# Attention projections in two row halves for units 4 to 15, one product for numerator and denominator in units 8 and 9, on one Trainium2 core

## The chip, the core and the metric

One of the eight cores of a Trainium2 chip runs the whole program. Its engines are TensorE (PE, with the loads of its stationary operand shown as PEld), VectorE (DVE), ScalarE (ACT), GpSimd (POOL) and SyncE (SP, which here issues DMAs). TensorE writes to PSUM, which has eight banks of 512 fp32 values in each of 128 partitions. The metric is the time on the device of one execution, in microseconds, as the median of several.

## The reference

Three layers follow one another: linear attention with positive random features, a gated MLP (in the code "moe"), and a soft mixture of experts ("moe2"). The change is in the first.

```
x = q * D**-0.25  (and k)                 # 4 batches, 8 heads, 576 tokens, D = 64
h = x @ omega.T - sum(x*x)/2              # 128 features
phi = exp(h - max(h)) / sqrt(128)
kv = phi(k).T @ v ;  z = sum(phi(k), tokens)
out = (phi(q) @ kv) / (phi(q) @ z + 1e-6)
x = out as 2304 tokens x 512
x = (sigmoid(x @ w_gate) * (x @ w_val)) @ w_out      # 1536 hidden
out = soft mixture of 8 experts with 4 slots each    # w1, w2 of 1024 hidden
```

## The kernel before

**Units.** A unit is two heads of one batch; there are 16. q and k come transposed, so a unit's tile has the two heads' 64 dimensions on 128 partitions and 1152 token columns (512 of k, a mixed tail tile of 64 of k and 64 of q, 512 of q). `chunk_proj` (L534) makes features of one or two tiles of 128 tokens: the token tile is the stationary operand and `obf` moves, omega of both heads as a block diagonal of 128 x 256, half of it zeros. One product gives both heads' 128 features. DVE then takes, per head and tile, the minimum of 128 features with the square sum added (`tensor_tensor_reduce`), ACT the exponential. The features lie in `HK`, `HT`, `HQ`, one buffer each. Five such calls make a unit.

**Precision.** For units 0 to 9 (`N_PROJ`, `N_NUM` = 10) these products are fp32; one appears as two records of TensorE, each streaming its columns twice. From unit 10 on q, k and omega are split into a high and a low fp32r part (`prep_qk`, L509), and `three` (L414) makes three passes of one record.

**After the projection.** `chunk_kv` (L559) sums features times v over the tokens, in 10 products a unit; v has ones beside it, so a head's 128 columns hold kv and z. `chunk_qT` (L573) turns the q features by TensorE: two calls with four 128 x 128 transposes and a third with two of the tail tile's 64 q rows (partitions 64 to 127). `chunk_num` (L589) is called for each half of the tokens (288). For units 0 to 9 it makes the denominators of both heads in one bank and the numerators in another, each by two products of 64 columns' width that write the two halves of the partitions. From unit 10 on one product of 128 columns gives numerator and denominator of a head.

**Banks.** `bank` (L496) hands out PSUM. While the first four units run, six tags serve attention; from then on (`wide[0]` false) attention and the moe2 chunks share the tag `fl` with two banks (`NFL = 2`). `ga`, `va` and `o0` to `o3` belong to the MLP.

**Order.** Nothing is issued directly. Each call is recorded by `Plan.add` (L136), and `Plan.schedule` (L213) runs a list schedule over the whole program with estimated costs (`cost`, L179), which fixes each engine's order, and for some operations the engine. A key taken from the job's due time and a lead per stream sets the priority. Each engine then runs its list in order and waits on semaphores. An operation on `fl` that finds no bank free is parked and offered again when one comes free.

**Stages.** Units 0 to 3 come first. Then the MLP runs in groups of steps over blocks of tokens (`GROUPS`, L32); a step is 12 matmuls each for `ga`, `va` and the `o` banks, fp32r, 512 columns. Units 4 to 7 lie among the first group, 8 to 11 among the second and third, 12 to 15 among the fourth; their outputs feed the MLP's later blocks. In the first two groups the MLP's weights are also converted from 64-bit floats (`convert`, L683) on ACT, DVE and POOL. `step_chunks` (L626) orders a unit's chunks: the sums of unit u, with the projection of unit u+1 in between.

Of the kernel before, what the change touches and what calls it, by code (L numbers as in the profile page):

```python
# [46 lines left out]
    "hqk": ("DVE", "ACT"), "lqk": ("POOL", "DVE"), "hqt": ("ACT", "DVE"),  # L47
# [9 lines left out]
N_PROJ = 10  # L57
# [28 lines left out]
HOP = 0.16  # L86

# [11 lines left out]
class Plan:  # L99


    def __init__(self, nc):
        self.eng = {"PE": nc.tensor, "ACT": nc.scalar, "DVE": nc.vector, "POOL": nc.gpsimd, "SP": nc.sync}
        self.ops = []
        self.tiles = {}
        self.tags = {}
        self.t = 0.0
        self.lead = {}
        self.floor = 0.0
        self.floors = []  # L110
        self.hist = {}

# [23 lines left out]
    def add(self, alts):  # L136
        _, method, args, kw = alts[0]
        outs = [kw[k] for k in ("out", "accum_out") if k in kw]
        ins = [v for k, v in kw.items() if k not in ("out", "accum_out") and hasattr(v, "tensor")]
        rest = [a for a in args if hasattr(a, "tensor")]  # L140
        if "out" not in kw and rest:
            outs.append(rest.pop(0))
        ins += rest
        i = len(self.ops)
# [24 lines left out]
        self.ops.append((alts, self.t - lead, preds, used, outs, ins, self.lead.get("lazy")))  # L169
# [9 lines left out]
    def cost(self, eng, method, kw, outs, ins):  # L179


        o = outs[0] if outs else None
# [30 lines left out]
    def schedule(self):  # L213
# [13 lines left out]
        dyn_of = [None] * n  # L227
        left = {}
        for tag, info in self.tags.items():
            gens = info["gens"]  # L230
            if info["dyn"]:
                for g, acc in enumerate(gens):
                    left[tag, g] = len(acc)
                    for a in acc:
                        dyn_of[a] = (tag, g)
# [86 lines left out]
        while ev:  # L322
            now = ev[0][0]
            while ev and ev[0][0] <= now + 1e-9:
# [3 lines left out]
                elif kind == 2:  # L328
                    d = dyn_of[x]
                    left[d] -= 1  # L330
                    if left[d] == 0:
                        room[d[0]] += 1
                        for p in parked[d[0]]:
                            offer(p)
                        parked[d[0]] = []
            for e in E:
                while free_at[e] <= now + 1e-9:
# [5 lines left out]
                    d = dyn_of[i]  # L343
                    if d and d not in live:
                        if room[d[0]] == 0:
                            if i not in parked[d[0]]:
                                parked[d[0]].append(i)
                            continue
                        room[d[0]] -= 1
                        live.add(d)  # L350
# [20 lines left out]
                    if d:  # L371
# [5 lines left out]
    def issue(self):  # L377
        for _, _, (e, method, a, k) in self.schedule():
            getattr(self.eng[e], method)(*a, **k)  # L379


def body(ctx, tc, nc, qkT, tok, von, omT, wall, phi, w1, w2, ident_d, srep_d, rrep_d, mask_d, out):
# [71 lines left out]
    q0, q1 = region(0, F32), half_region(0, F32)  # L454
# [3 lines left out]
    QT = KV = XK = XQ = obh = obl = None  # L458

    def split_regions():  # L460

        nonlocal QT, KV, XK, XQ, obh, obl
        g0, g1 = region(0, F32R), half_region(1, F32R)
        QT = carve(g0, 0, [2, 2, S])
        KV = carve(g0, 2304, [2, 2, 128])
        XK = carve(g0, 2816, [2, 640])
        XQ = carve(g1, 0, [2, 512])
        obh = carve(g1, 1024, [256])
        obl = carve(g1, 1280, [256])
        hi_of(obh, obf, ("DVE",))  # L470
        lo_of(obl, obf, obh, ("DVE",))
# [6 lines left out]
    HK = carve(g4, 0, [4, 2, M])  # L478
    HQ = carve(g4, 1024, [4, 2, M])
    HT = carve(g4, 2048, [1, 2, M])  # L480
# [5 lines left out]
    MX = [carve(g4, 3730 + 8 * k, [2, 4]) for k in range(6)]  # L486
# [22 lines left out]
    def prep_qk(u, kind):  # L509
# [3 lines left out]
        if u == N_PROJ and kind == 0:  # L513
            split_regions()
        x, c, t, n = ((XK, slice(0, 640), 0, 5), (XQ, slice(640, 1152), 5, 4))[kind]
        src = QKTs[u % 2][:, c]
# [16 lines left out]

    def chunk_proj(u, i):  # L534

        if u >= NU:
            return
        x, c0, nt, hb, g0 = ((XK, 0, 2, HK[:, 0:2], 0), (XK, 256, 2, HK[:, 2:4], 4), (XK, 512, 1, HT, 8),
                             (XQ, 0, 2, HQ[:, 0:2], 10), (XQ, 256, 2, HQ[:, 2:4], 14))[i]
        ps = bank()  # L540
        psv = ps.rearrange("p (t m) -> p t m", t=2)
        for t in range(nt):
            c = slice(c0 + 128 * t, c0 + 128 * t + 128)
            if u < N_PROJ:
                PE.matmul(psv[:, t], QKTs[u % 2][:, 640 * (i > 2) + c0 + 128 * t:][:, 0:128], obf, start=True, stop=True)
            else:
                three(psv[:, t], (x[:, 0, c], x[:, 1, c]), (obh, obl))
        n = 2 * nt
        sq = SQ[:, g0:g0 + n]
        flat = ps.rearrange("p (g m) -> p g m", m=M)[:, 0:n, :]  # L550
        hv = hb.rearrange("p t h m -> p (t h) m")
        low = turn(MX, "mx")[:, 0, 0:n]
        for g in range(n):
            DVE.tensor_tensor_reduce(out=hv[:, g], in0=flat[:, g], in1=sq[:, g:g + 1].to_broadcast([128, M]),
                                     scale=1.0 / 16.0, scalar=BIG, op0=ALU.add, op1=ALU.min, accum_out=low[:, g:g + 1])
        for g in range(n):
            ACT.activation(out=hv[:, g], in_=hv[:, g], func=AF.Exp, scale=-1.0, bias=low[:, g:g + 1])

    def chunk_kv(u):  # L559

        ps = bank()[:, 0:256].rearrange("p (h c) -> p h c", h=2)
        for h in range(2):
            for t in range(NT):
                k = HK[:, t, h, :] if t < 4 else HT[:, 0, h, :]
# [8 lines left out]
    def chunk_qT(u, i):  # L573
        ps = bank().rearrange("p (h n) -> p h n", h=2)
        n = (256, 256, 64)[i]
        for h in range(2):
            if i == 2:
                PE.transpose(ps[:, h, 0:64], HT[64:128, 0, h, :], ident[64:128, 64:128])
                continue
            for t in range(2):  # L580
                PE.transpose(ps[:, h, 128 * t:128 * t + 128], HQ[:, 2 * i + t, h, :], ident)
        if u < N_NUM:
            copy(QTF[:, :, 256 * i:256 * i + n], ps[:, :, 0:n], SITE["hqt"])
            return
        qh, ql = (QT[:, l, :, 256 * i:256 * i + n] for l in range(2))
        hi_of(qh, ps[:, :, 0:n], SITE["hqt"])
        lo_of(ql, ps[:, :, 0:n], qh, ("DVE",))

    def chunk_num(u, half):  # L589
# [4 lines left out]
        if u < N_NUM:  # L594
# [8 lines left out]
        else:  # L603
            pn = []
            for h in range(2):
                ps = bank()[:, 0:HALF]
                pn.append(ps)
                three(ps, (KV[:, 0, h, :], KV[:, 1, h, :]), (QT[:, 0, h, c:c + HALF], QT[:, 1, h, c:c + HALF]))
                ACT.activation(out=R[num[h]], in_=ps[den[h]], func=AF.Ln, bias=den_b[den[h]])
# [16 lines left out]
    def step_chunks(u):  # L626
# [11 lines left out]
        def last():  # L638
            chunk_proj(v, 4)
            prep_qk(u + 2, 0)  # L640

        c = [kv, P(0), lambda: chunk_qT(u, 0), P(1), lambda: chunk_qT(u, 1), lambda: chunk_qT(u, 2), P(2),
             lambda: chunk_num(u, 0), P(3), lambda: chunk_num(u, 1), last]
        own = (0, 2, 4, 5, 7, 9)
# [444 lines left out]
    chunk_proj(0, 0)  # L1089
    prep_first(2, 5)  # L1090
    prep_qk(0, 1)
    chunk_proj(0, 1)
    chunk_proj(0, 2)
    SP.dma_start(out=TOK, in_=tok[1])
    SP.dma_start(out=Vs[1], in_=von[1])
    chunk_proj(0, 3)
    chunk_proj(0, 4)
# [186 lines left out]
```

## Time and profile before

| | us |
|---|---|
| median of 3 runs | 703.87 |
| lowest, highest | 703.55, 704.65 |
| the profiled execution: its span, first to last instruction | 702.4 |
| PE busy | 678.3 |
| PEld busy | 543.9 |
| DVE busy | 445.7 |
| ACT busy | 443.1 |
| POOL busy | 301.3 |

The profiled execution has no time of its own beside its span. All computing instructions are issued at line L379, so groups are told apart by the names of tiles: `fl<-g,g` is attention work, `ga`, `va` and `o` with `XT,w` or `gt,w` are the MLP. Busy time of PE is modelled at its ends, so the starts of successive records tell more than their durations.

### The profile page before, as it was taken

The numbers are of one execution on the slowest core, as the hardware profiler recorded it, in microseconds if no ns is written. First come the engines' busy times: TensorE is split into PE (matmuls) and PEld (weight loads), VectorE is DVE, ScalarE is ACT, GpSimd is POOL, SyncE is SP. The second block draws the span as 40 slices with busy tenths as digits, with TensorE's granted clock in tenths as the row PEclk, the third lists the DMA queues.
The fourth block names the chain that finished last, engine by engine and source line by source line (L and its number), as shares of the span: only waits on it lengthen the run. The fifth ranks groups of instructions, "written<-read, shape, count | busy, mean of one in ns | idle before, by whom it ended". The sixth has DMA issues, their size and how long they took to land.

```text
span 702.4 us, 12029 instructions
## 1 busy us (share of the span) xinstructions
PE 678.3 (97%) x4095; PEld 543.9 (77%) x4095; DVE 445.7 (63%) x1292; ACT 443.1 (63%) x987; POOL 301.3 (43%) x255
## 2 busy tenths in 40 slices
PE   8999999999989999999999999999999999999993
PEld 6677667777767788788888888778888788998662
DVE  4898997899997554657476765555454335766221
ACT  5999898888777565856567674654444444765021
POOL 0356545546454444644444444354444444642000
PEclk9999999999999999999999999999999999999998
DMA  7878777677866335443333334469422228557897
GB/s 279 297 253 308 249 229 255 227 257 271 267 238 201 123 114 206 148 133 108 133 135 132 90 115 142 127 231 330 166 91 90 91 83 281 168 162 250 320 407 235
DMA packets 50124, 139.47 MB, mean 199 GB/s; under 512 B 5520, under 2 KB 11152, under 8 KB 50064
## 3 DMA queue, kind: packets, MB, share of 16 engines
q1 hardware_dynamic: 45456, 121.94, 51.9%
q10 hardware_dynamic: 4608, 16.78, 6.9%
q8 instruction: 32, 0.52, 0.3%
q14 instruction: 28, 0.23, 0.1%
HBM read 124.54 MB, written 14.16 MB: 197 GB/s over the span
## 4 chain that ended last, share of the span: by engine, by line
PE 67%; DVE 4%; issue 3%; ACT 2%; DMA 2%; POOL 1%; POOLq 0%; ACTq 0%; DVEq 0%
PE o L379 19%; PE ga L379 18%; PE va L379 18%; PE fl L379 12%; DVE x2T L379 2%; DMA ws<-wscr 1%; DVE g L379 1%; DVE ga_a L379 1%; ACT ga_a L379 1%; DMA g<-in_wall 1%; POOL w L379 1%; ACT g L379 0%; ACT XT L379 0%; ACT gt L379 0%; ACT x2T L379 0%
## 5 line engine op out<-in xcount | busy, mean ns | idle before, releaser
L379 POOL TENSOR_TENSOR w<-ws,w 128x512 fp32r<-128x512 f32 x141 | 188.3, 1336 | 235.7 <-ACT w L379 132.5
L379 PE MATMUL ga<-XT,w 128*128 128x512 f32 (+1 forms) x720 | 169.4, 377 | 1.8 <-DVE ga_a L379 1.0
L379 PE MATMUL va<-XT,w 128*128 128x512 f32 (+1 forms) x720 | 167.6, 376 | 1.2 <-DVE ga_a L379 1.2
L379 PE MATMUL o<-gt,w 128*128 128x512 f32 (+1 forms) x720 | 165.3, 374 | 0.9 <-ACT w L379 0.8
L379 PEld LDWEIGHTS ga<-XT,w 128*128 128x128 f32 x720 | 123.8, 189 | 28.1 <-issue 3.0
L379 PEld LDWEIGHTS va<-XT,w 128*128 128x128 f32 x720 | 123.5, 189 | 27.1 <-issue 3.7
L379 PEld LDWEIGHTS o<-gt,w 128*128 128x128 f32 x720 | 123.6, 189 | 25.1 <-issue 2.6
L379 ACT ACTIVATE g<-g 128x128 f32<-128x128 f32 (+3 forms) x340 | 121.1, 415 | 18.9 <-DVE g L379 12.9
L379 ACT ACTIVATE w<-ws 128x512 fp32r<-128x512 f32 x107 | 67.3, 629 | 61.9 <-issue 19.8
L379 PE MATMUL fl<-g,g 128*128 128x128 f32 (+2 forms) x514 | 87.8, 343 | 3.2 <-DVE g L379 2.1
L379 PEld LDWEIGHTS fl<-g,g 128*128 128x128 f32 (+1 forms) x514 | 61.8, 179 | 22.5 <-issue 6.6
L379 ACT ACTIVATE ga_a<-ga_a 128x512 f32<-128x512 f32 (+1 forms) x120 | 70.2, 585 | 12.6 <-DVE ga_a L379 11.5
L379 ACT ACTIVATE ga_a<-ga 128x512 f32<-128x512 f32 (+1 forms) x60 | 33.2, 554 | 65.4 <-PE ga L379 65.3
L379 DVE CUSTOM_DVE_ANT_0 g<-fl,g 128x128 f32<-128x128 f32 x242 | 56.9, 286 | 19.5 <-PE fl L379 19.0
L379 DVE SCALAR_TENSOR_TENSOR ga_a<-ga,ga_a 128x512 f32<-128x512 f32 (+1 forms) x60 | 38.2, 636 | 46.4 <-ACT ga_a L379 46.1
L379 DVE CAST w<-ws 128x512 fp32r<-128x512 f32 x55 | 23.8, 432 | 67.8 <-PE ga L379 38.1
L379 ACT ACTIVATE x2T<-g 128x512 f32<-128x512 f32 x72 | 45.9, 670 | 5.8 <-DVE x L379 5.7
L379 DVE TENSOR_SCALAR x2T<-x2T 128x512 f32<-128x512 f32 (+1 forms) x72 | 47.7, 670 | 0.9 <-ACT x2T L379 0.8
L379 DVE TENSOR_TENSOR ga_a<-va,ga_a 128x512 f32<-128x512 f32 (+1 forms) x60 | 38.0, 634 | 15.3 <-ACT ga_a L379 11.9
L379 POOL TENSOR_TENSOR XT<-g,XT 128x288 fp32r<-128x288 f32 (+2 forms) x46 | 31.3, 690 | 32.0 <-ACT XT L379 29.5
L379 ACT ACTIVATE ga_a<-ga_a,one_b 128x512 f32<-128x512 f32 (+1 forms) x60 | 40.8, 679 | 1.2
L379 DVE TENSOR_TENSOR g<-fl,g 64x288 f32<-64x288 f32 (+3 forms) x57 | 27.6, 485 | 15.5 <-ACT g L379 12.5
(200 smaller groups left out, 752.6 us busy)
## 6 DMA issues: line engine op xcount, KB each, us to landing
ws<-wscr SPq DMA_DIRECT2D x42, 512.0 KB, 3.6
ws<-wscr SPq DMA_DIRECT2D x78, 256.0 KB, 2.8
g<-in_wall SPq DMA_DIRECT2D x36, 512.0 KB, 4.9
g<-in_von SPq DMA_DIRECT2D x16, 640.0 KB, 5.1
wscr<-x SPq DMA_DIRECT2D x36, 256.0 KB, 4.5
g<-in_qkT SPq DMA_DIRECT2D x15, 576.0 KB, 4.8
g<-in_tok SPq DMA_DIRECT2D x15, 576.0 KB, 5.0
g<-in_w ACTq DMA_DIRECT2D x16, 512.0 KB, 5.2
```

What stands on the lines that cost most here:

```text
L379: getattr(self.eng[e], method)(*a, **k)
```

## The change

From unit 4 on (`ROWS = 4`), the four full tiles of k (and of q) of both heads are projected in one call as eight fp32 products with 64 rows each: head 0 from partitions 0 to 63, head 1 from 64 to 127, 128 columns each, in two banks, one for each head. The tail tile stays one block-diagonal product. The split of q, k and omega for units 10 to 15 is dropped; their projections are fp32. Units 0 to 3 keep the old calls under new names. Features have two sets of buffers that alternate by unit (the second in the region `g1b`). The tail tile is transposed whole, and only its q columns are copied. Units 8 and 9 make numerator and denominator of a head as one fp32 product, in two banks. `together` records several products as one bundle for the planner: they are ordered as a block, and need all their banks free at once. An operation on `fl` now also parks behind one with an earlier key. Three prices of the planner change.

```diff
+TURN = 0.2
+ROWS = 4
+WHOLE = 8
+    def together(self, calls, first=(), then=()):
+        self.bundle = []
+        calls()
+        parts, self.bundle = self.bundle, None
+        self.place([(parts[0][0][0], "together", (), {"parts": parts})],
+                   [o for _, outs, _ in parts for o in outs] + list(then),
+                   [i for _, _, ins in parts for i in ins] + list(first))
...
             if o.ap[0][1] == 64:
-                return max(n / 600.0, 0.21) / 2 + 0.02, False
-            return (0.416 if ins[0].ap[0][1] == 64 else max(0.222, n / 600.0)), False
+                return max(n / 600.0, 0.21) / 2 + 0.12, False
+            return (max(0.222, n / 600.0) / 2 if ins[0].ap[0][1] == 64 else max(0.222, n / 600.0)), False
...
             if method == "tensor_tensor_reduce":
-                return 0.16 + ni / 960.0, False
+                return 0.075 + ni / 960.0, False
...
-                    if d and d not in live:
-                        if room[d[0]] == 0:
+                    fresh = [d for d in dyn_of[i] if d not in live]
+                    if fresh:
+                        tag = fresh[0][0]
+                        first = any(ops[q][1] < ops[i][1] for q in parked[tag])
+                        if room[tag] < len(fresh) or first:
...
-        if u >= N_PROJ:
-            hi_of(x[:, 0, :], src, SITE["hqk"])
-            lo_of(x[:, 1, :], src, x[:, 0, :], SITE["lqk"])
...
+        def products():
+            for t in range(nt):
+                if nt < 4:
+                    PE.matmul(both[:, t].rearrange("p h m -> p (h m)"), x[:, 128 * t:128 * t + 128], obf,
+                              start=True, stop=True)
+                    continue
+                for h in range(2):
+                    r = slice(64 * h, 64 * h + 64)
+                    PE.matmul(ps[h][:, t], x[r, 128 * t:128 * t + 128], obf[r, 128 * h:128 * h + 128],
+                              start=True, stop=True)
+        plan.together(products, [SQ[:, g0:g0 + 2 * nt]], [hb])
...
-                PE.transpose(ps[:, h, 0:64], HT[64:128, 0, h, :], ident[64:128, 64:128])
+                PE.transpose(ps[:, h, 0:128], HTs[u % 2][:, 0, h, :], ident)
...
-        if u < N_NUM:
+        if u < WHOLE:
...
+                    if u < N_NUM:
+                        PE.matmul(pn[h], KVF[:, h], QTF[:, h, c:c + HALF], start=True, stop=True)
...
+        if v < ROWS:
+            c = [kv, P("K0"), qT[0], P("K1"), qT[1], qT[2], P("T"), num[0], P("Q0"), num[1], last]
+        else:
+            c = [kv, P("K"), qT[0], qT[1], qT[2], P("T"), num[0], num[1], last]
```

## Rows read from the trace of the kernel before

**Rows 1.** The page: busy time of each engine, share of the span, instructions

```profile
PE 678.3 (97%) x4095; PEld 543.9 (77%) x4095; DVE 445.7 (63%) x1292; ACT 443.1 (63%) x987; POOL 301.3 (43%) x255
```

**Rows 2.** Stretches: length, busy time of each engine, granted clock, DMA

```profile
core 0: us, PE busy (x) PEld busy (x) DVE busy (x) ACT busy (x) POOL busy (x), PEclk, DMA share, GB/s
0.00:40.00 40.00, 36.41 (x194) 27.20 (x194) 26.28 (x138) 30.63 (x88) 11.21 (x16) 1.00 0.80 282
60.00:160.00 100.00, 98.18 (x499) 71.91 (x499) 86.56 (x265) 87.78 (x212) 50.92 (x46) 1.00 0.75 249
160.00:200.00 40.00, 36.93 (x166) 29.61 (x165) 38.62 (x63) 30.21 (x58) 20.97 (x15) 1.00 0.74 253
200.00:470.00 270.00, 268.83 (x1467) 220.67 (x1466) 166.53 (x502) 176.99 (x384) 124.97 (x105) 1.00 0.44 146
470.00:640.00 170.00, 168.82 (x1020) 146.28 (x1020) 90.84 (x185) 87.70 (x167) 80.80 (x63) 1.00 0.51 167
```

**Rows 3.** PE in order of time (start, length, names, shapes, count): bare groups

```profile
469.82 2.88 PE L379 MATMUL ga<-XT,w 128*128 128x512 f32 x12
472.54 2.88 PE L379 MATMUL va<-XT,w 128*128 128x512 f32 x12
```

**Rows 4.** PE in order of time: transposes, then two old projection tiles in fp32

```profile
188.28 0.60 PE L379 MATMUL fl<-ident,g 128*128 128x128 f32 x4
188.63 3.02 PE L379 MATMUL va<-XT,w 128*128 128x512 f32 x12
191.49 1.02 PE L379 MATMUL fl<-g,g 128*128 128x256 f32 x4
192.16 3.12 PE L379 MATMUL o<-gt,w 128*128 128x512 f32 x12
195.12 0.60 PE L379 MATMUL fl<-ident,g 128*128 128x128 f32 x4
```

**Rows 5.** PE in order of time: features times v, then fp32r projection tiles

```profile
342.70 2.39 PE L379 MATMUL fl<-g,g 128*128 128x128 f32 x20
344.85 2.98 PE L379 MATMUL ga<-XT,w 128*128 128x512 f32 x12
347.66 0.88 PE L379 MATMUL fl<-g1b,g 128*128 128x256 f32 x6
348.38 2.91 PE L379 MATMUL va<-XT,w 128*128 128x512 f32 x12
351.13 0.60 PE L379 MATMUL fl<-ident,g 128*128 128x128 f32 x4
```

**Rows 6.** PE in order of time, products of 64 columns' width; a group of their loads

```profile
244.70 1.19 PE L379 MATMUL fl<-g,g 128*64 128x288 f32 x8
245.82 3.02 PE L379 MATMUL va<-XT,w 128*128 128x512 f32 x12
248.68 0.88 PE L379 MATMUL fl<-g1b 128*128 128x256 f32 x6
...
L379 PEld LDWEIGHTS fl<-g,g 128*64 128x64 f32 x120 | 6.2, 135 | 11.1 <-issue 5.6 <-DVE g L379 2.2 <-ACT g L379 1.6
```

**Rows 7.** PE in order of time: transposes of a 64-row half

```profile
235.47 2.99 PE L379 MATMUL va<-XT,w 128*128 128x512 f32 x12
238.40 0.33 PE L379 MATMUL fl<-ident,g 64*128 64x64 f32 x2
238.66 3.01 PE L379 MATMUL o<-gt,w 128*128 128x512 f32 x12
241.51 0.52 PE L379 MATMUL fl<-g1b,g 128*128 128x256 f32 x3
```

**Rows 8.** Groups on DVE and ACT (busy us, mean ns); PE's waits (us, times, longest)

```profile
L379 DVE CUSTOM_DVE_ANT_0 g<-fl,g 128x128 f32<-128x128 f32 x242 | 56.9, 286 | 19.5 <-PE fl L379 19.0
L379 DVE TENSOR_TENSOR g<-fl,g 64x288 f32<-64x288 f32 x24 | 10.9, 454 | 5.8 <-ACT g L379 3.1 <-PE ga L379 2.3
L379 ACT ACTIVATE g<-fl,den_b 64x288 f32<-64x288 f32 x24 | 12.0, 499 | 1.6 <-PE fl L379 0.9
PE fl L379 <- DVE g L379: 5.2, 9, 1.8
```

More of the change, by code (lines that the diff above doesn't have):

```diff
@@ L46 @@
 SITE = {
-    "hqk": ("DVE", "ACT"), "lqk": ("POOL", "DVE"), "hqt": ("ACT", "DVE"),
+    "hqt": ("ACT", "DVE"),
     "hx": ("ACT", "DVE"), "lx": ("POOL", "DVE"), "hg": ("DVE", "ACT"),
@@ L56 @@
 T0 = -60
-N_PROJ = 10
+N_SPLIT = 10
 N_NUM = 10
@@ L111, in __init__ @@
         self.hist = {}
+        self.bundle = None
+    def together(self, calls, first=(), then=()):
[5 more added lines that the diff above has]
+                   [i for _, _, ins in parts for i in ins] + list(first))
     def tile(self, pool, shape, dtype, tag, bufs=1, dyn=False):
@@ L143, in add, with place @@
         ins += rest
+        if self.bundle is not None:
+            self.bundle.append((alts[0], outs, ins))
+        else:
+            self.place(alts, outs, ins)
+    def place(self, alts, outs, ins):
         i = len(self.ops)
@@ L179, in cost @@
     def cost(self, eng, method, kw, outs, ins):
+        if method == "together":
+            return TURN * (kw["parts"][0][2][0].ap[0][1] == 64) + sum(self.cost(eng, a[1], a[3], o, i)[0] for a, o, i in kw["parts"]), False
         o = outs[0] if outs else None
@@ L226, in schedule @@
         nv = n
-        dyn_of = [None] * n
+        dyn_of = [[] for _ in range(n)]
         left = {}
@@ L234, in schedule @@
                     for a in acc:
-                        dyn_of[a] = (tag, g)
+                        dyn_of[a].append((tag, g))
                 continue
@@ L328, in schedule @@
                 elif kind == 2:
[L329 to L335, printed above, removed]
+                    for d in dyn_of[x]:
+                        left[d] -= 1
+                        if left[d] == 0:
+                            room[d[0]] += 1
+                            for p in parked[d[0]]:
+                                offer(p)
+                            parked[d[0]] = []
             for e in E:
@@ L342, in schedule @@
                     backlog[p[0]] -= self.cost(p[0], p[1], p[3], ops[i][4], ops[i][5])[0]
-                    d = dyn_of[i]
-                    if d and d not in live:
-                        if room[d[0]] == 0:
-                            if i not in parked[d[0]]:
-                                parked[d[0]].append(i)
+                    fresh = [d for d in dyn_of[i] if d not in live]
[3 more added lines that the diff above has]
+                        if room[tag] < len(fresh) or first:
+                            if i not in parked[tag]:
+                                parked[tag].append(i)
                             continue
-                        room[d[0]] -= 1
-                        live.add(d)
+                        room[tag] -= len(fresh)
+                        live.update(fresh)
                     alts, _, _, _, outs, ins, lazy = ops[i]
@@ L378, in issue @@
         for _, _, (e, method, a, k) in self.schedule():
-            getattr(self.eng[e], method)(*a, **k)
+            for e, method, a, k in [p[0] for p in k["parts"]] if method == "together" else [(e, method, a, k)]:
+                getattr(self.eng[e], method)(*a, **k)
 def body(ctx, tc, nc, qkT, tok, von, omT, wall, phi, w1, w2, ident_d, srep_d, rrep_d, mask_d, out):
@@ L457, in body @@
     part = carve(q1, 0, [4, 512])
-    QT = KV = XK = XQ = obh = obl = None
+    QT = KV = None
     def split_regions():
-        nonlocal QT, KV, XK, XQ, obh, obl
-        g0, g1 = region(0, F32R), half_region(1, F32R)
+        nonlocal QT, KV
+        g0 = region(0, F32R)
         QT = carve(g0, 0, [2, 2, S])
         KV = carve(g0, 2304, [2, 2, 128])
[L466 to L471, printed above, removed]
     QKTs = [carve(g2, 1152 * k, [1152]) for k in range(2)]
@@ L477, in body @@
     obf = carve(g3, 3712, [256])
-    HK = carve(g4, 0, [4, 2, M])
-    HQ = carve(g4, 1024, [4, 2, M])
-    HT = carve(g4, 2048, [1, 2, M])
+    HKs = [carve(r, 0, [4, 2, M]) for r in (g4, q2)]
+    HQs = [carve(r, 1024, [4, 2, M]) for r in (g4, q2)]
+    HTs = [carve(g4, at, [1, 2, M]) for at in (2048, 3792)]
     RR = [carve(g4, 2304 + 288 * k, [HALF]) for k in range(2)]
@@ L485, in body @@
     SQ = carve(g4, 3712, [18])
-    MX = [carve(g4, 3730 + 8 * k, [2, 4]) for k in range(6)]
+    MX = [carve(g4, 3730 + 8 * k, [8]) for k in range(6)]
     ring = {}
@@ L512, in prep_qk @@
             return
-        if u == N_PROJ and kind == 0:
+        if u == N_SPLIT and kind == 0:
             split_regions()
-        x, c, t, n = ((XK, slice(0, 640), 0, 5), (XQ, slice(640, 1152), 5, 4))[kind]
-        src = QKTs[u % 2][:, c]
-        if u >= N_PROJ:
-            hi_of(x[:, 0, :], src, SITE["hqk"])
-            lo_of(x[:, 1, :], src, x[:, 0, :], SITE["lqk"])
+        t, n = ((0, 5), (5, 4))[kind]
         w = SQW[:, 0:2 * n, :]
@@ L532, in prep_first @@
         DVE.tensor_reduce(out=SQ[:, 2 * a:2 * e], in_=w, axis=AX.X, op=ALU.add)
+    PARTS = {"K": (0, 4, HKs, 0, 0), "K0": (0, 2, HKs, 0, 0), "K1": (256, 2, HKs, 2, 4),
+             "T": (512, 1, HTs, 0, 8), "Q": (640, 4, HQs, 0, 10), "Q0": (640, 2, HQs, 0, 10), "Q1": (896, 2, HQs, 2, 14)}
     def chunk_proj(u, i):
@@ L537, in chunk_proj @@
             return
[L538 to L557, printed above, removed]
+        c0, nt, hb, t0, g0 = PARTS[i]
@@ new lines, in chunk_proj @@
+        hb = hb[u % 2][:, t0:t0 + nt]
+        x = QKTs[u % 2][:, c0:c0 + 128 * nt]
+        if nt < 4:
+            both = bank()[:, 0:256 * nt].rearrange("p (t h m) -> p t h m", h=2, m=M)
+            ps = [both[:, :, h] for h in range(2)]
+        else:
+            ps = [bank()[:, 0:128 * nt].rearrange("p (t m) -> p t m", m=M) for _ in range(2)]
+        def products():
+            for t in range(nt):
+                if nt < 4:
+                    PE.matmul(both[:, t].rearrange("p h m -> p (h m)"), x[:, 128 * t:128 * t + 128], obf,
[5 more added lines that the diff above has]
+                              start=True, stop=True)
@@ new lines, in chunk_proj @@
+        plan.together(products, [SQ[:, g0:g0 + 2 * nt]], [hb])
+        low = turn(MX, "mx")
+        for h in range(2):
+            for t in range(nt):
+                g = 2 * t + h
+                DVE.tensor_tensor_reduce(out=hb[:, t, h], in0=ps[h][:, t],
+                                         in1=SQ[:, g0 + g:g0 + g + 1].to_broadcast([128, M]),
+                                         scale=1.0 / 16.0, scalar=BIG, op0=ALU.add, op1=ALU.min,
+                                         accum_out=low[:, g:g + 1])
@@ L559, in chunk_kv @@
+        for h in range(2):
+            for t in range(nt):
+                g = 2 * t + h
+                ACT.activation(out=hb[:, t, h], in_=hb[:, t, h], func=AF.Exp, scale=-1.0, bias=low[:, g:g + 1])
     def chunk_kv(u):
@@ L574, in chunk_qT @@
         ps = bank().rearrange("p (h n) -> p h n", h=2)
-        n = (256, 256, 64)[i]
+        n, k = ((256, 0), (256, 0), (64, 64))[i]
         for h in range(2):
             if i == 2:
-                PE.transpose(ps[:, h, 0:64], HT[64:128, 0, h, :], ident[64:128, 64:128])
+                PE.transpose(ps[:, h, 0:128], HTs[u % 2][:, 0, h, :], ident)
                 continue
             for t in range(2):
-                PE.transpose(ps[:, h, 128 * t:128 * t + 128], HQ[:, 2 * i + t, h, :], ident)
+                PE.transpose(ps[:, h, 128 * t:128 * t + 128], HQs[u % 2][:, 2 * i + t, h, :], ident)
         if u < N_NUM:
-            copy(QTF[:, :, 256 * i:256 * i + n], ps[:, :, 0:n], SITE["hqt"])
+            copy(QTF[:, :, 256 * i:256 * i + n], ps[:, :, k:k + n], SITE["hqt"])
             return
         qh, ql = (QT[:, l, :, 256 * i:256 * i + n] for l in range(2))
-        hi_of(qh, ps[:, :, 0:n], SITE["hqt"])
-        lo_of(ql, ps[:, :, 0:n], qh, ("DVE",))
+        hi_of(qh, ps[:, :, k:k + n], SITE["hqt"])
+        lo_of(ql, ps[:, :, k:k + n], qh, ("DVE",))
     def chunk_num(u, half):
@@ L603, in chunk_num, with products @@
         else:
-            pn = []
+            pn = [bank()[:, 0:HALF] for _ in range(2)]
+            def products():
+                for h in range(2):
+                    if u < N_NUM:
+                        PE.matmul(pn[h], KVF[:, h], QTF[:, h, c:c + HALF], start=True, stop=True)
+                    else:
+                        three(pn[h], (KV[:, 0, h, :], KV[:, 1, h, :]), (QT[:, 0, h, c:c + HALF], QT[:, 1, h, c:c + HALF]))
+            plan.together(products)
             for h in range(2):
[L606 to L609, printed above, removed]
+                ACT.activation(out=R[num[h]], in_=pn[h][den[h]], func=AF.Ln, bias=den_b[den[h]])
             ACT.activation(out=R, in_=R, func=AF.Exp, scale=-1.0)
@@ L638, in last @@
         def last():
-            chunk_proj(v, 4)
+            chunk_proj(v, "Q1" if v < ROWS else "Q")
             prep_qk(u + 2, 0)
-        c = [kv, P(0), lambda: chunk_qT(u, 0), P(1), lambda: chunk_qT(u, 1), lambda: chunk_qT(u, 2), P(2),
-             lambda: chunk_num(u, 0), P(3), lambda: chunk_num(u, 1), last]
-        own = (0, 2, 4, 5, 7, 9)
+        qT = [lambda i=i: chunk_qT(u, i) for i in range(3)]
+        num = [lambda i=i: chunk_num(u, i) for i in range(2)]
+        if v < ROWS:
+            c = [kv, P("K0"), qT[0], P("K1"), qT[1], qT[2], P("T"), num[0], P("Q0"), num[1], last]
+            own = (0, 2, 4, 5, 7, 9)
+        else:
+            c = [kv, P("K"), qT[0], qT[1], qT[2], P("T"), num[0], num[1], last]
+            own = (0, 2, 3, 4, 6, 7)
         if v >= NU:
@@ L1088, in body @@
     prep_first(0, 2)
-    chunk_proj(0, 0)
+    chunk_proj(0, "K0")
     prep_first(2, 5)
     prep_qk(0, 1)
-    chunk_proj(0, 1)
-    chunk_proj(0, 2)
+    chunk_proj(0, "K1")
+    chunk_proj(0, "T")
     SP.dma_start(out=TOK, in_=tok[1])
     SP.dma_start(out=Vs[1], in_=von[1])
-    chunk_proj(0, 3)
-    chunk_proj(0, 4)
+    chunk_proj(0, "Q0")
+    chunk_proj(0, "Q1")
     prep_qk(1, 0)
```

6 lines of the change are left out of this document (3 added, 3 removed).

## The prediction, made before the result was known

> **What bounds the kernel now.** I read the page first, then the stretches, then the order of instructions on TensorE. The busy row [rows 1] shows PE at 97% of the span; no other engine passes 63%, apart from the weight loads, which run beside PE. That is an average, so the stretches come next [rows 2]. From 200 to 470 us PE is busy 268.8 of 270 us, with DVE at 166.5 and ACT at 177.0: here PE alone sets the pace. From 60 to 160 us PE is busy 98.2 of 100, but DVE (86.6) and ACT (87.8) are close behind. From 160 to 200 us DVE is busy 38.6 of 40 and PE has gaps: DVE sets the pace. Before 40 us PE has gaps too (36.4 of 40). The granted clock is 1.00 up to 640 us, the higher level, so no price below needs a clock correction. Attention ends at about 470 us [rows 3]; what follows is the same code on the same data and costs nothing either way.
>
> So the change is priced in PE time, and PE time is read from starts, since the ends are modelled. A bare group of 12 MoE matmuls takes 472.54 - 469.82 = 2.72 us [rows 3]. A visit of attention work between two groups costs the distance from its start to the end of the next group, less 2.72.
>
> **The prices.** An fp32 matmul appears as two records. Two token tiles of the old projection (four records, 256 columns): 195.12 - 191.49 - 2.72 = 0.91 us; four transposes: 191.49 - 188.28 - 2.72 = 0.49 [rows 4]. Ten fp32 products of 128 columns (20 records): 347.66 - 342.70 - 2.72 = 2.24, so 0.112 a record; two token tiles in three fp32r passes (six records): 351.13 - 347.66 - 2.72 = 0.75 [rows 5].
>
> A visit in another shape of the array costs a turn. Eight records of 64 columns' width and 288 columns' length: 248.68 - 244.70 - 2.72 = 1.26 [rows 6]. Two transposes of a 64-row half: 241.51 - 238.40 - 2.72 = 0.39; the group ahead of it is late as well, 2.93 us (238.40 - 235.47) [rows 7] against 2.86 (191.49 - 188.63) ahead of a visit in the full shape [rows 4], so 0.07 is added to each: 1.33 and 0.46. The eight records stream 288 columns twice each, 0.24 us at 2.4 GHz. One after the other that would be 1.92; they took 1.33, so the two column halves run side by side in four steps (0.96), and the turn is 0.37. The transposes give about the same, 0.46 less 0.05 to 0.11 of work. The weight loads of the column halves overlap too: 6.2 us busy for 120 of 135 ns each [rows 6].
>
> "TensorEngine Tiling (Array Packing)", § Key Properties, in the Trainium skill says that changing the tiling mode drains TensorE. It speaks against this change, which adds 24 such visits. The trace agrees with 0.37 us a visit. With no turn the 24 bundles would save 24 x 0.3 = 7 us more, and the 18 visits that go (6 of narrow products, 12 of tail transposes) 5 us less.
>
> **The change part by part.** *Projection of units 4 to 9.* Four visits of 0.91 (3.64) become two of eight products each, in two row halves, 128 columns long. The trace has no two row halves side by side. Bounds: side by side as the column halves, 8 steps of 0.112 plus 0.37 = 1.27 a visit; one after the other, 16 x 0.112 + 0.37 = 2.16. I take 1.27, because the nearest row, the column halves, shows both streams and loads overlapping. Two visits 2.53, the tail tile unchanged: -1.11 a unit, x6 = -6.6 (upper bound +0.69 a unit, +4.1).
>
> *Projection of units 10 to 15.* Four visits of 0.75 and a tail of half that (0.38), 3.38 in all, become 2.53 plus a tail of 0.46: -0.39 a unit, x6 = -2.3 (upper bound +1.41 a unit, +8.4). The splits of q and k into two parts go from DVE, ACT and POOL. I count them at nothing, since behind 200 us PE is the bound; bounds 0 and -1.
>
> *Numerator and denominator of units 8 and 9.* Unit 8 makes four visits of four records (0.48 + 0.37 = 0.85 each, 3.40), unit 9 two of eight (2.66). Each becomes two visits of four full-width records, 4 x 0.24 + 0.06 (an ordinary visit's surplus, 0.91 - 4 x 0.213) = 1.02, so 2.04 a unit: -1.4 and -0.6, together -2.0. On ACT each of four halves has two logarithms in place of one, 0.5 us more each, and on DVE two products, 0.45 more [rows 8]: 2.0 and 1.8 us, hidden behind PE in 200 to 260 us; without that cover they cost 2.
>
> *The tail transposes of every unit* are done whole: 0.25 (half of four) for 0.46, -0.21 a unit, x12 = -2.5 for units 4 to 15. In units 0 to 3 they lie before 60 us and I count none.
>
> *Second feature buffers, one order bound together, new planner prices.* These change only what may run when. The planner's DVE price for a projection piece falls from 0.293 to 0.208 us; the trace has 56.9/242 = 0.235 busy [rows 8]. The start has PE gaps of 3.6 us in 40 [rows 2]: bounds -2 to +2, I take 0, because ACT (30.6 of 40, its exponentials unchanged) is what works there.
>
> *What is added as a wait.* Both halves write separate banks, and the shared pool has two. A bundle starts only with both free, and other users of that pool queue behind it; PE takes MoE work meanwhile unless the order already has the bundle next. Bounds: 0, or the emptying of one bank more, 4 x 0.235 = 0.94 us for each of 24 bundles, +22.6. PE now waits for that pool's readers 5.2 us in 9 waits [rows 8] over the whole run, so I take 0 and keep the upper end as a rival.
>
> **The sum.** -6.6 - 2.3 - 2.0 - 2.5 = -13.4 us of PE time. Of it 6.4 falls before 160 us (five projections at 1.11, four tail transposes), 7.0 after. Where PE is alone the bound nearly all arrives: 90%, -6.3. Before 160 us, taking 6.4 out of 100 us puts ACT and DVE at 87.8 and 86.6 of 93.6, and a PE that queues behind engines this full waits more; I take 55%, -3.5. Together -9.8: the span of 702.4 us becomes 692.6. The median of the runs, 703.87, is 1.47 above the profiled span, so **694.1 us**.
>
> **Rivals.** *Halves in turn.* If the row halves don't overlap, the upper bounds hold: +4.1 + 8.4 - 2.0 - 2.5 = +8.0, 711.9 us. For: no row of before shows them together. Against: column halves do. In the Trainium skill, "TensorE: Matmul & The Clock Gate", § Part 3: Packing small matmuls, says that weight loads overlap matmuls in flight only when the row group differs. Taken strictly, a load would wait for its own half's stream and a visit would cost about the same 2.1 us. The trace does not bear that out in the full shape, where 0.112 a record leaves no room for load and stream in sequence.
>
> *The two-bank wait.* From 0.41 us a bundle on average (9.8/24) the gain is gone; at 0.6 the time is 703.9 - 9.8 + 14.4 = 708.5. For: in-order PE, two banks, DVE full before 200 us. Against: only 5.2 us of such waits now.
>
> *The elementwise engines become the bound.* Nothing is kept before 200 us and some of the rest goes: -5, about 699. For: DVE 38.6 of 40 us. Against: between 60 and 160 us both still have 12 us in 100.
>
> *All of it arrives*, with a better order at the start: -13.4 to -16, 688 to 690.5.
>
> **Chances.** Forecast 0.58 (its own range 690.5 to 698), elementwise bound 0.16, all of it 0.08, halves in turn 0.10, two-bank wait 0.08. What no measurement of this kernel can tell from none is 0.2%, 1.4 us. Faster takes the forecast, all of it, and most (0.13) of the elementwise case: 0.79; within 0.2% gets 0.02 of that case and 0.02 of the two-bank one, 0.04; slower the rest, 0.17. The range 688 to 708 leaves out the serial case, half of the two-bank one and the end of the best one, under 0.2.
>
> **What would show it.** In the profile after: 384 records of 64 rows and 128 columns in pairs starting close together, a bundle's 16 records over about 0.9 us and its visit 1.3; single records 0.11 apart would be the serial case. The 64-row transposes and the 64-wide products of units 8 and 9 are gone. The bare groups that follow attention begin some 10 us earlier, and the time behind them is as before. PE's waits for the shared banks stay near 5 us. The prediction fails if the bundles take over 1.8 us, or if those waits pass 10 us.

## The result, and the profile after

The changed kernel takes 693.68 us (median of 6 runs, 692.74 to 696.61). The kernel before, run beside it, takes 703.71. The ratio is 0.9862, with a 95% interval of 0.9834 to 0.9889: 9.7 us less, where 9.8 was forecast. Runs of these two kernels differ mostly with the clock: at a mean granted clock of 0.995 or more the changed kernel's spans are 690.9 to 691.2 us and those of the kernel before, run beside the experiments, 699.3 to 700.4, so 8 to 9.5 us lie between them there. The profiled execution of the changed kernel is the longest of its six (696.61 us, span 694.8), so from span to span the traces differ by 7.6 us; why is told below.

The page's busy row of the changed kernel, then its stretches (length, busy time of each engine, granted clock, DMA); their counterparts are [rows 1] and [rows 2]:

```profile
PE 668.5 (96%) x4217; PEld 535.4 (77%) x4217; DVE 459.4 (66%) x1304; ACT 433.1 (62%) x968; POOL 288.4 (42%) x244
```

```profile
60.00:160.00 100.00, 96.85 (x573) 70.44 (x574) 94.86 (x284) 86.47 (x207) 53.48 (x47) 1.00 0.74 249
160.00:200.00 40.00, 38.79 (x192) 31.60 (x191) 39.39 (x70) 32.35 (x63) 17.74 (x13) 1.00 0.80 272
200.00:460.00 260.00, 257.78 (x1470) 210.89 (x1469) 167.31 (x492) 165.72 (x367) 108.83 (x93) 1.00 0.44 144
```

Behind 200 us PE is still full. From 60 to 160 us DVE rose from 86.6 to 94.9 of 100 us. Part of it is work that lies there now: 80 projection pieces for 72, and eight copies of 512 columns out of the shared banks for four (ACT made four others before, now none). Over the whole run DVE is busy 13.7 us more, ACT 10.0 and POOL 12.9 less. Between 160 and 200 us PE works more than before, 38.8 for 36.9.

The bundle, with the bare groups around it, in order of time on PE:

```profile
247.70 2.88 PE L403 MATMUL ga<-XT,w 128*128 128x512 f32 x12
250.51 1.16 PE L403 MATMUL fl<-g,g 64*128 64x128 f32 x16
251.61 3.02 PE L403 MATMUL va<-XT,w 128*128 128x512 f32 x12
254.46 0.38 PE L403 MATMUL fl<-g,g 128*128 128x128 f32 x2
...
338.84 2.98 PE L403 MATMUL ga<-XT,w 128*128 128x512 f32 x12
341.75 1.16 PE L403 MATMUL fl<-g,g 64*128 64x128 f32 x16
```

A visit costs 254.46 - 250.51 - 2.72 = 1.23 us. The group ahead is late too: 2.81 us here, 2.91 to 2.93 ahead of the other four bundles that follow a whole group (341.75 - 338.84). Against 2.86 ahead of a visit in the full shape, as the prediction counts it, that adds some 0.05: 1.28. That is 30% less than the two visits of 0.91 each in [rows 4]. The group lines say how: 384 records of the new shape and the loads beside them, busy time and mean of one.

```profile
L403 PE MATMUL fl<-g,g 64*128 64x128 f32 x384 | 29.2, 285 | 0.2 <-DVE g L403 0.2
L403 PEld LDWEIGHTS fl<-g,g 64*128 64x128 f32 x384 | 24.5, 187 | 8.9 <-issue 3.6 <-DVE g L403 2.8 <-DVE x L403 0.4
```

Full-width fp32 records of 128 columns follow each other at 0.112 us [rows 5], so 384 of them in single file would take 43 us. These took 29.2. In 19 of the 24 bundles all pairs start together; five run 1.26 to 1.45 us for 1.09.

The whole tail transposes, then the joint product of unit 9 (240.20) in the changed kernel, against [rows 7] and [rows 6]:

```profile
267.04 2.99 PE L403 MATMUL o<-gt,w 128*128 128x512 f32 x12
269.87 0.38 PE L403 MATMUL fl<-ident,g 128*128 128x128 f32 x2
270.01 3.01 PE L403 MATMUL ga<-XT,w 128*128 128x512 f32 x12
272.86 0.39 PE L403 MATMUL va<-XT,w 128*128 128x512 f32 x1
...
237.25 3.12 PE L403 MATMUL ga<-XT,w 128*128 128x512 f32 x12
240.20 1.13 PE L403 MATMUL fl<-g,g 128*128 128x288 f32 x4
240.96 0.84 PE L403 MATMUL va<-XT,w 128*128 128x512 f32 x2
```

Two transposes now cost 272.86 - 269.87 - 2.72 = 0.27 us, where it was 0.46. A joint product starts 0.76 us ahead of the next group; the eight narrow records started 1.12 ahead. One of the four joint products waits, though:

```profile
205.98 2.65 PE L403 MATMUL va<-XT,w 128*128 128x512 f32 x11
210.27 1.31 PE L403 MATMUL fl<-g,g 128*128 128x288 f32 x4 [1.64 <-DVE g L403]
211.20 0.61 PE L403 MATMUL va<-XT,w 128*128 128x512 f32 x1
```

It needs both shared banks. They hold the other half's results, whose DVE products stood behind a 1.77 us conversion of weights and a step of 0.68 after it in DVE's order. PE's waits of this kind, over the whole run (us, times, longest), counterpart [rows 8]:

```profile
PE fl L403 <- DVE g L403: 7.5, 10, 1.7
```

Where the time went shows in a landmark that both kernels pass, the records of the logits of a block. Before, for the first and the last block that has 32 of them in a shared bank, and for the last block of all, which has 16 in `ga`:

```profile
293.57 1.08 PE L379 MATMUL fl<-x2T,phs 128*32 128x128 f32 x32 [0.22 <-DVE g L379]
...
591.07 1.08 PE L379 MATMUL fl<-x2T,phs 128*32 128x128 f32 x32
L379 PE MATMUL ga<-x2T,phs x16: 272/273/297, 643.7 to 645.0; 128*32 128x128 f32 x16
```

and after:

```profile
287.03 1.08 PE L403 MATMUL fl<-x2T,phs 128*32 128x128 f32 x32 [0.33 <-DVE g L403]
...
583.35 1.08 PE L403 MATMUL fl<-x2T,phs 128*32 128x128 f32 x32
L403 PE MATMUL ga<-x2T,phs x16: 272/273/297, 634.4 to 635.7; 128*32 128x128 f32 x16
```

6.5 us are gained by the first, 7.7 by the second, 9.3 by the third (643.7 for 634.4). Then 1.7 are lost again, in work that is the same. The stretches there, of the kernel before and then of the changed one, have PE busy throughout and the clock below its higher level for longer in the changed kernel:

```profile
650.00:655.00 5.00, 5.00 (x45) 3.60 (x48) 1.26 (x4) 0.00 (x0) 0.00 (x0) 0.66 0.70 265
```

```profile
640.00:645.00 5.00, 5.00 (x40) 4.21 (x43) 1.46 (x6) 0.00 (x0) 0.00 (x0) 0.68 0.74 297
645.00:650.00 5.00, 5.00 (x68) 2.36 (x64) 0.48 (x1) 0.00 (x0) 0.00 (x0) 0.63 0.93 297
```

Counted by MLP records on PE, the 217th (the first behind the first group) starts at 149.05 for 149.76, the 325th at 174.48 for 179.06. By 150 us 0.7 had arrived, and one projection visit that the changed kernel is ahead by then: attention's records had taken 80.5 us for 84.8, but PE had waited 9.7 us for 5.8. Of the next four, 1.2 are two waits of the kernel before that are not there after; the rest is attention work that stands elsewhere in the order.

### The profile page after: what moved, and what is told of

It reads as the page before. It is cut to its first block, busy times and chain, and to the rows that moved or that the text cites. A ratio compares the mean times of both kernels' runs of the same rounds, so it can differ in the third digit from the quotient of the medians.

```text
span 694.8 us, 12218 instructions
## 1 busy us (share of the span) xinstructions
PE 668.5 (96%) x4217; PEld 535.4 (77%) x4217; DVE 459.4 (66%) x1304; ACT 433.1 (62%) x968; POOL 288.4 (42%) x244
## 4 chain that ended last, share of the span: by engine, by line
PE 79%; DVE 8%; DMA 5%; ACT 3%; issue 3%; SPq 1%; POOL 0%; POOLq 0%; ACTq 0%; DVEq 0%
PE o L403 25%; PE ga L403 20%; PE va L403 19%; PE fl L403 15%; DVE x2T L403 3%; DVE g L403 2%; DMA ws<-wscr 2%; DMA g<-in_wall 2%; DVE x L403 1%; ACT g L403 1%; DMA wscr<-x 1%; DMA g<-in_tok 1%; ACT ga_a L403 1%; SPq L403 1%; DVE gt L403 1%
## 5 line engine op out<-in xcount | busy, mean ns | idle before, releaser
L403 POOL TENSOR_TENSOR w<-ws,w 128x512 fp32r<-128x512 f32 x138 | 181.6, 1317 | 254.1 <-ACT w L403 156.4
L403 PE MATMUL o<-gt,w 128*128 128x512 f32 (+1 forms) x720 | 167.8, 377 | 0.9 <-ACT w L403 0.8
L403 PE MATMUL fl<-g,g 64*128 64x128 f32 (+4 forms) x686 | 84.1, 313 | 4.8 <-DVE g L403 4.2
L403 ACT ACTIVATE g<-g 128x128 f32<-128x128 f32 (+3 forms) x204 | 73.4, 410 | 15.3 <-DVE g L403 9.7
L403 PEld LDWEIGHTS fl<-g,g 64*128 64x128 f32 (+2 forms) x686 | 61.0, 183 | 26.7 <-DVE g L403 9.4
L403 ACT ACTIVATE g1b<-g1b,g 128x128 f32<-128x128 f32 x128 | 40.5, 390 | 8.6 <-DVE g L403 8.6
L403 DVE TENSOR_SCALAR x2T<-x2T 128x512 f32<-128x512 f32 (+1 forms) x72 | 44.0, 627 | 1.0 <-ACT x2T L403 1.0
L403 DVE TENSOR_TENSOR gt<-ga_a,gt 128x512 fp32r<-128x512 f32 (+1 forms) x53 | 40.3, 760 | 2.3 <-ACT gt L403 1.3
L403 DVE TENSOR_TENSOR g<-fl,g 64x288 f32<-64x288 f32 (+3 forms) x61 | 29.3, 482 | 17.4 <-ACT g L403 16.5
```

## The experiments

Each is the changed kernel with the edit shown, unless it says otherwise; ratios are to the kernel before, run on the same chip. The changed kernel itself stands at 0.9862, and 0.01 is 7 us. A difference of two such ratios is uncertain by 2.5 to 3 us.

**Halves in turn.** Order of products within a bundle:

```diff
-            for t in range(nt): ... for h in range(2):
+            for h in range(2): for t in range(nt):
```

> The changed kernel (693.7 us) with one order reversed: a bundle makes all four tiles of head 0 first and then all four of head 1, so neighbouring records lie in the same row half. Same products, banks, bundles and planner prices. Theory (the gain comes from two row halves at work at once): a bundle's 16 records take 16 x 0.112 = 1.8 us and not 0.9, 24 bundles cost 21.5 us more of PE time, and 70 to 90% of it arrives: 709 to 713 us, slower than the kernel before (703.7). Rival (the gain comes from fewer visits and from the new order of the whole program, and the halves overlap in either order): 692 to 697 us.

1.003 (1.0013 to 1.0046), 705.0 us: 11.8 us slower than the changed kernel. Only the order within a bundle differs, so overlap is shown. The bundle is this, on PE:

```profile
250.89 2.88 PE L403 MATMUL ga<-XT,w 128*128 128x512 f32 x12
253.70 1.71 PE L403 MATMUL fl<-g,g 64*128 64x128 f32 x16
255.34 3.03 PE L403 MATMUL va<-XT,w 128*128 128x512 f32 x12
```

It runs 1.64 us from its start to the next group, where the changed kernel's runs 1.10. The expectation of 1.8 for the records alone was too high: in the middle of the bundle three records of head 1 start 0.004 to 0.006 us after one of head 0, so 13 steps are made and not 16. That is up to 24 x 0.54 = 13 us of PE time, and the runs are 11.8 us longer. In the trace, of the shortest of its twelve runs, the projections' records take 11.4 us more and the logits in `ga` start 8.3 us later.

**No row halves.**

```diff
-ROWS = 4
+ROWS = 16
```

> The changed kernel with the row halves undone for all units: every projection is the block-diagonal fp32 product in five calls, units 10 to 15 too; buffers, transposes, products of units 8 and 9 and prices stay. Theory: each of 12 units pays 4 x 0.91 for 2 x 1.27, 1.1 us, 13 us of PE time in all, of which 9 to 12 arrive: 703 to 706 us, so the row halves carry nearly the whole gain. Rival (transposes, second buffers, prices carry most of it): 695 to 699 us.

0.9994 (0.9975 to 1.0013). The whole gain is gone, as expected. This kernel also pays fp32 in units 10 to 15 (4 x 0.91 + 0.46 for 3.38, 4.3 us), which about eats what transposes and joint products give.

**Row halves from unit 10 on only.**

```diff
-ROWS = 4
+ROWS = 10
```

> The changed kernel with the row halves for units 10 to 15 alone; units 4 to 9, most of which lie before 160 us, have the block-diagonal product again: 6.6 us of PE time come back. Theory (before 160 us about half of PE time shows as time): 697 to 698.5 us. Rival one (DVE, busy 94.9 of 100 us there in the changed kernel, is the bound, PE time counts for little): 693.5 to 695.5 us. Rival two (PE alone is the bound everywhere): 700 us.

0.9911 (0.9885 to 0.9936): 3.4 us slower than the changed kernel, for 6.6 us of PE time. About half, as the theory said; the first rival ends where this interval begins, the second lies outside. The traces show less: the projections' records take 4.9 us more, PE waits 4.8 us less, and the logits in `ga` start 0.7 us later. That PE time is partly hidden there is shown, how much of it stays open.

**Units 8 and 9 as before.**

```diff
-WHOLE = 8
+WHOLE = 10
```

> The changed kernel with units 8 and 9 back at separate products of 64 columns' width for denominator and numerator. Theory (turns of 0.37 us for six visits): 2 us of PE time come back, 695 to 696 us. Rival (the joint products wait for their inputs about as long as the turns took, as one gap of 2.0 us ahead of such a product in the trace suggests): 693 to 694.5 us.

0.9902 (0.9879 to 0.9926): 2.8 us slower, little more than the uncertainty. By the runs the joint products are worth about what the turns said. The traces show less: the records of these products take 1.4 us more here, and from the 324th to the 648th MLP record, where units 8 and 9 lie, 99.0 us pass for 98.4. So the rival, that the wait at 210 us takes back most of it, is not refuted.

**Tail transposes from the half.**

```diff
-                PE.transpose(ps[:, h, 0:128], HTs[u % 2][:, 0, h, :], ident)
+                PE.transpose(ps[:, h, 0:64], HTs[u % 2][64:128, 0, h, :], ident[64:128, 64:128])
```

> The changed kernel (0.986 of the kernel before) with the tail's q rows transposed from the 64-row half again. Theory: 12 visits behind 60 us cost 0.21 us more each, 2.5 us of PE time, of which about 2 arrive: 0.989 of the kernel before. Rival (the turn into a shape is paid anyway by neighbouring bundles): 0.985 to 0.987.

0.9905 (0.9876 to 0.9933): 3.0 us slower, near the 2 expected, within its interval. Part of it is not the transposes: in its trace, of the longest of its six runs, 2.1 of the 3.8 us lost by the logits in `ga` are there by the 217th MLP record, and the clock is 0.72 from 15 to 20 us, behind a wait of 3.6 us, which is 1.7 us in the changed kernel.

**Joint products from unit 4 on.**

```diff
-WHOLE = 8
+WHOLE = 4
```

> The changed kernel with units 4 to 7 as well making numerator and denominator of a head as one product. PE saves about 1 us a unit, 4 us; ACT gets 16 x 0.5 = 8 us more and DVE 16 x 0.45 = 7 us more, all between 60 and 160 us, where the changed kernel's DVE is busy 94.9 of 100. Theory (with the changed kernel DVE and ACT bound that stretch): no gain or a loss, 0.986 to 0.992. Rival (PE alone is the bound there): 0.980 to 0.983.

0.9982 (0.9966 to 0.9998): 8.4 us slower, although PE has less to do. The first stretch and then two of 5 us:

```profile
60.00:160.00 100.00, 89.87 (x519) 69.42 (x521) 94.31 (x276) 90.35 (x210) 50.71 (x44) 0.97 0.77 255
150.00:155.00 5.00, 1.67 (x5) 0.92 (x5) 4.87 (x11) 4.90 (x11) 1.18 (x2) 0.93 0.93 301
155.00:160.00 5.00, 2.62 (x15) 1.76 (x15) 4.16 (x8) 3.83 (x9) 3.19 (x4) 0.50 1.00 347
```

PE stands idle for 10 us of the 100 with DVE busy 94 and ACT 90: before 160 us they are the bound. The second effect is in the clock column. Behind a wait of 3.33 us PE's granted clock is 0.50, the lower level, and a second wait, of 2.38 us, follows in that stretch.

**The old price in the planner.**

```diff
-                return 0.075 + ni / 960.0, False
+                return 0.16 + ni / 960.0, False
```

> The changed kernel with the planner's old price for the projection's DVE pieces (0.293 us for 0.208). The work is the same, the order of all engines is planned anew. Theory (prices were counted at nothing): 0.983 to 0.989. Rival (the truer price gave part of the gain): 0.990 or more.

0.9976 (0.9951 to 1.0): 8.0 us slower with the same operations, planned anew. My theory fell here. On PE:

```profile
209.40 2.65 PE L403 MATMUL va<-XT,w 128*128 128x512 f32 x11
215.18 2.29 PE L403 MATMUL fl<-g,g 128*128 128x288 f32 x4 [3.13 <-DVE g L403]
216.85 1.04 PE L403 MATMUL va<-XT,w 128*128 128x512 f32 x1
217.69 4.49 PE L403 MATMUL o<-gt,w 128*128 128x512 f32 x12
222.03 1.55 PE L403 MATMUL ga<-XT,w 128*128 128x512 f32 x6
```

and the stretches of 5 us there:

```profile
210.00:215.00 5.00, 2.05 (x10) 1.36 (x8) 5.00 (x7) 3.06 (x7) 2.38 (x2) 0.92 0.55 209
215.00:220.00 5.00, 4.82 (x11) 3.67 (x12) 3.60 (x7) 3.95 (x8) 0.82 (x1) 0.50 0.49 157
```

The joint product that waits 1.64 us in the changed kernel waits 3.13 here, and the clock falls to 0.50: a bare group of 12 takes 222.03 - 217.69 = 4.34 us and not 2.72. Another wait, of 1.93 us near 181 us, is followed by a clock of 0.81 over the next 5. The order planned from the old price puts PE behind DVE at two places, and it pays for the wait and again for the clock: the logits in `ga` start 7.1 us later, PE waits 2.2 us more, and the MLP's records take 4.5 us more.

**Products planned one by one.**

```diff
-        plan.together(products, [SQ[:, g0:g0 + 2 * nt]], [hb])
+        products()
```

> The changed kernel with the projection's products planned one by one, not as a bundle: a product needs one bank, and other work may come between the two halves of a pair. Theory (waiting for two banks costs little, and visits cut into pieces pay more turns): 0.986 to 0.995, with more visits to the 64-row shape in the trace. Rival (the wait for both banks holds the changed kernel back): 0.983 or less.

1.0126 (1.0098 to 1.0154): 18.6 us slower than the changed kernel, more than expected.

```profile
107.32 0.40 PE L403 MATMUL va<-XT,w 128*128 128x512 f32 x1
107.65 1.16 PE L403 MATMUL fl<-g,g 64*128 64x128 f32 x8
108.73 0.73 PE L403 MATMUL va<-XT,w 128*128 128x512 f32 x2
...
114.43 0.39 PE L403 MATMUL o<-gt,w 128*128 128x512 f32 x1
114.75 1.16 PE L403 MATMUL fl<-g,g 64*128 64x128 f32 x8
115.83 0.50 PE L403 MATMUL o<-gt,w 128*128 128x512 f32 x1
```

The planner takes one bank when it is free, so one head goes alone: 8 records take 1.08 us to the next group, where a bundle's 16 take 1.10. 13 of the 24 bundles fall apart into two such visits in single file, 37 visits in all. This is the rival of halves in turn, brought about by the order. Here too the joint product waits 3.5 us and the clock falls to 0.50.

**The new price in the kernel before.** The same line, in the kernel before:

```diff
-                return 0.16 + ni / 960.0, False
+                return 0.075 + ni / 960.0, False
```

> The kernel before with one number changed: the planner's price of a projection piece on DVE is 0.208 us for 0.293. The changed kernel with the old price took 0.998 of the kernel before, so either the price is worth about 8 us by itself, or only together with the bundles. Theory (together: the price tells the planner how soon a bundle's two banks are free, which the old projection, one bank at a time, hardly asks): 0.995 to 1.003. Rival (by itself): 0.985 to 0.991.

1.0048 (1.0027 to 1.0069): the price is no gain by itself, rather a small loss beyond the expected bound. In these two pairs of runs it counts only together with the bundles.

**One set of feature buffers.**

```diff
-    HKs = [carve(r, 0, [4, 2, M]) for r in (g4, q2)]
+    HKs = [carve(r, 0, [4, 2, M]) for r in (g4, g4)]     # HQs and HTs likewise
```

> The changed kernel with one set of feature buffers again, as before: a bundle's features can be written only when the unit before has been summed and transposed. Theory (a change of what may run when, counted at nothing): 0.984 to 0.989. Rival (a bundle holds both shared banks until its features are written, so waiting for the one buffer holds the banks and the work behind them): 0.992 or more.

1.0059 (1.0035 to 1.0082): 14 us slower, as much as the rival said. Its reason, banks held while they wait, is not shown. The first 60 us, with one set and then in the changed kernel:

```profile
0.00:60.00 60.00, 46.62 (x260) 37.07 (x261) 48.09 (x207) 46.78 (x127) 17.48 (x22) 0.97 0.93 335
```

```profile
0.00:60.00 60.00, 53.15 (x313) 39.88 (x314) 44.76 (x221) 47.76 (x136) 26.07 (x29) 1.00 0.84 293
```

PE is busy 6.5 us less, and the first bundle starts at 63.4 us instead of 52.3. The new code orders a projection only when its feature buffer is free. That this is the link, and not another part of the new order, is argued from the code.

**Integer adds to POOL.**

```diff
-    "add": ("DVE", "POOL"),
+    "add": ("POOL", "DVE"),
```

> The changed kernel with the integer add of the weight conversion put to POOL first and DVE second. DVE, busy 94.9 of 100 us between 60 and 160 us, gives up some 20 adds of 0.78 us, POOL (53 of 100) takes them at 1.29. Theory (DVE is the bound of that stretch since the change): 0.979 to 0.984. Rival (the conversion's chain gets longer and POOL delays the splits of the weights behind it): 0.988 or more.

0.9869 (0.9842 to 0.9896), no difference from the changed kernel. The theory's range ends just below the interval, the rival's begins within it. DVE falls to 88.4 of 100 us from 60 to 160 us, and ACT stays at 87.6. By the runs DVE's busy time alone is not the bound there. Its trace, of the shortest of its six runs, does have 4.3 us less of PE's waits than the changed kernel's, so what the bound is, DVE and ACT in turn or single waits, stays open.

**Row halves from unit 2 on.**

```diff
-ROWS = 4
+ROWS = 2
```

> The changed kernel with the row halves from unit 2 on. Units 2 and 3 are projected before 55 us, where PE has gaps. Theory (ACT's exponentials, unchanged in number, set the start): 0.984 to 0.989, no change. Rival (the shorter visits shorten the start): 0.982 or less.

0.9931 (0.9907 to 0.9955): 4.9 us slower than the changed kernel, which neither side expected. Again PE has a gap, and the clock falls behind it:

```profile
45.00:50.00 5.00, 3.29 (x26) 2.20 (x28) 5.00 (x33) 4.53 (x14) 0.37 (x1) 0.85 0.89 294
50.00:55.00 5.00, 5.00 (x36) 3.67 (x33) 3.68 (x11) 4.47 (x15) 3.09 (x4) 0.80 0.61 211
```

No variant beat the changed kernel. Every edit but the first has the planner order the whole program anew, and orders of the same operations differ by up to 8 us here (the old price). So a difference of 3 us can't be put down to the edited part alone.

## Why the prediction was right, point by point

*What bounds the kernel.* Right behind 200 us, where PE time removed is time gained: halves in turn put 11 to 13 us of PE time in over the whole run, and 11.8 arrived in the runs, 8.3 in the trace. Before 160 us DVE and ACT stand close behind, as read; joint products from unit 4 on made PE idle 10 us in 100.

*The visit of the halves.* 1.27 was forecast from the column halves, 1.28 measured. The turn that they showed, 0.37 us, held for the new shape (1.28 less eight steps of 0.112).

*The sum.* -13.4 us was nearly right as PE time of attention, and too much as time. Summing from each record's start to the next one's, waits apart, up to the logits in `ga`, the projections give 50.1 for 58.7 (-8.6; forecast -8.9), the transposes of q features -2.6 (-2.5), the products of numerator and denominator -1.6 (-2.0) and other work -0.6. Against them the MLP's records take 2.1 more, where the late start ahead of a bundle and the first record behind it are booked, and PE waits 13.1 for 11.1, 2.0 more. That is the -9.3 at this place.

*What arrives, and where.* 55% before 160 us and 90% behind it gave 9.8, and 9.7 came, but not by these shares. In this trace under 2 us had arrived by 150 us, not 3.5: the waits rose almost as much as PE time fell. 1.5 of the 9.3 came behind the last attention work, where nothing was forecast; one wait of 1.05 us of the kernel before is not there after. The groups that follow attention begin 7.7 us earlier and not some 10, and the time behind them hides two changes: those 1.5, and the 1.7 that the clock takes back in this trace. That the total is met to 0.1 us is luck. For units 4 to 9 the share was tested: 3.4 of 6.6 us in the runs, less in the traces.

*The step that failed: buffers, bundle and prices "I take 0", bounds -2 to +2.* Taken away singly they cost 14 us (buffers), 18.6 (bundle) and 8.0 (price). The price gives nothing by itself, as the new price in the kernel before shows; buffers and bundle were not tried there. With the new work, the PE time saved arrives only if the order keeps PE from waiting. I priced them by what they remove from an engine, which is nothing, and not by what the new work needs from them. With all three there the 0 did no harm; each run without one of them (707.2, 713.4 and 701.8 us) lies outside the forecast's 690.5 to 698.

*The two-bank wait.* 7.5 us in 10 waits for 5.2 in 9, below the 10 that would have refuted it. 1.64 of it lies at the joint product of unit 8 and 1.71 at a product of features times v near 86 us; of the bundles of the projection one waits, 0.22 us. The rival was closer than it looked: with 1.5 us more at that place the clock falls as well.

*Rivals.* Halves in turn did not happen, but two of the experiments made it happen, one of them in part, and both were slower than the kernel before. The elementwise engines hold PE back before 150 us, where its waits rose by 3.9 us, but 6.0 us are gained by the 433rd MLP record (206.0 for 211.9), so the rival that keeps nothing before 200 us did not happen. The row halves' loads and streams overlap as the column halves' did in [rows 6]. The Trainium skill's rule on loads ("TensorE: Matmul & The Clock Gate", § Part 3: Packing small matmuls) does not hold taken strictly: with halves in turn, records of the same half still follow each other at 0.112 us.

## What to carry to other kernels

A price for a new tile shape can be read from another shape that splits the array as well: take the turn and the overlap from starts, with the edges of the visit on both sides. Edits that only decide order have to be priced by what the new work asks of them: which banks and buffers it needs at once, who empties them, and what stands ahead of that in the emptying engine's list. Two row halves help only while neighbouring instructions lie in different halves.

## What the runs showed of the hardware

Short waits of PE cost twice. In seven of the twelve variants the granted clock of some stretch of 5 us between 10 and 630 us is below 0.9, in the two kernels compared it is in none. The shown ones follow gaps: 0.50 behind a wait of 3.13 us, where a group of 2.72 us took 4.34. The changed kernel's wait of 1.64 us at the same place left the clock at 1.00, but with one set of buffers it is 0.66 from 70 to 75 us behind a wait of 1.29 us. Not every fall follows a wait: behind 640 us it falls in both kernels compared with PE busy throughout. Records of the two row halves start 0.006 to 0.010 us apart in 19 of the 24 bundles, and steps follow at 0.112. With one head's products all first, PE still took three records of the other half beside those of the first.
